# Moving weight divisions and input loads within the first expert group of a recurrence-plus-mixture kernel

## The chip, the cores and the metric

The kernel runs on one core of a Trainium2 chip. The metric is the device time of one execution in microseconds. Three runs of the kernel before took 970.49, 967.85 and 964.76 us, a median of 967.85 us.

The core's engines have their own instruction queues, which run in order: PE (TensorE, the matrix engine), DVE (VectorE), ACT (ScalarE), POOL (GpSimd) and SP (SyncE, which here only issues DMAs). They wait for each other through semaphores. DMAs are issued by SP (queue q1 in the profile) and by POOL (queue q0).

## The reference

Two blocks follow each other. The first is a gated linear recurrence over 768 steps for 4 batches and 8 heads of size 48; its output, put into rows of 384, goes to a mixture of four experts with plain weights.

```python
for t in range(S):
    state = alpha[:, :, t, :, None] * state + np.einsum('bhd,bhe->bhde', k[:, :, t], v[:, :, t])
    y[:, :, t] = np.einsum('bhd,bhde->bhe', q[:, :, t], state)
x = y.transpose(0, 2, 1, 3).reshape(B * S, H * D)          # 3072 x 384
p = domain_probs / (domain_probs.sum(-1, keepdims=True) + 1e-09)
for e in range(E):                                          # 4 experts
    h = np.maximum(x @ w1[e], 0.0)                          # 384 -> 1024
    out += p[:, e:e + 1] * (h @ w2[e])                      # 1024 -> 384
```

## The kernel before

**Units and groups.** The 3072 rows are 24 units of 128 tokens (4 batches times 6 blocks of the sequence). A unit's recurrence is done as attention over pairs of tokens, in seven levels (`attention`, L531 on): transposes of alpha, k and q on PE (`turned`, L336), copies of them on ACT (L548, L556), products of the levels on PE (L622, L698, L703), with ACT (L585, L594, L614) and DVE (L601, L603, L615) preparing each level from the one before, then the result (`yps`, L743) and the new state (`sps`, L776), for which the keys are turned back (transpose L336, copy `AT<-tp` L760). The first unit has its own function, `first_unit`, which keeps its seven stages of queries and keys in tiles that later hold weights: `places` cuts the four `w1` and four `w1s` tiles into 16 of them.

Units are put in groups: the first has 2, then come five of 4 and a last one of 2. For each group and each expert, `up` makes the hidden rows with w1 (L864 or L870) in eight steps `fc`, and `down` makes the output rows with w2 (L956). The attention of the next group runs between these matmuls. In the first group the experts go round by one (`real`): expert 1, 2, 3, then 0.

**Weights in two parts.** From the third expert of the first group on, matmuls use a rounded type, and every weight and activation is the sum of a top and a rest: three matmuls instead of one. A weight's *division* (`split_piece`) takes a raw piece of 384 KB: ACT makes the top (L294, 128x768), DVE subtracts it to give the rest (L296, 128x768), then POOL stores the two to DRAM (`kept`, L302, 768 KB for w1), from where later groups load them. The third part is a short copy that POOL loads straight from the weights, converting on the way (`load_short`, L234: `w1s` for w1, `w` for w2). The store is left out for the pieces of w2 that are divided in the first group. There are four pieces (`NQ`) to each weight of each expert.

**What sets the order.** The program is written out by hand (`manual_schedule`): the order in which the functions run is the order on every queue. Three helpers thread work into it:

- `making` is a queue of divisions. Each call of `background()`, one after each step of `up` and every few matmuls of `down`, moves every running division on by one `yield` and starts one more (at most four run).
- `BEATS`, `deal` and `advance` say at which share of a unit's time slot each of its 18 steps is issued; for the second group the last five beats have values of their own. The third of these is the beat of turning the keys back.
- `load` and `load_piece` issue the inputs of a unit and the raw weights on SP at the places where they are called.

**The parts that the change touches, as they stand before.** In `first_unit`, the third unit's alpha is loaded after the first unit's keys are copied, then piece 0 of the first w1, k, piece 1, q, pieces 2 and 3. At the first step of `up` for the first expert, SP issues four pieces of w2 and then `p_all`, the probabilities. The last expert's w1 is divided in the second layer of the third expert (`down(0, 2)`, two pieces for each of two units), followed there by pieces 0 and 1 of its w2; pieces 2 and 3 of that w2 are divided at steps 0 and 2 of its own first layer (`up(0, 3)`). The raw w2 for it (tile `raw`) is loaded at the end of `up(0, 2)`. In time, `up(0, 2)` runs from about 78 to 91 us, `down(0, 2)` to 106, `up(0, 3)` to 120 and `down(0, 3)` to 134.

Of the kernel before, what the change touches and what calls it, by code (L numbers as in the profile page):

```python
# [10 lines left out]
F32 = mybir.dt.float32  # L11
# [9 lines left out]
def kernel(  # L21
# [40 lines left out]
    E, DM, F = moe_w1.shape  # L62
    P = 128
    NCB = S // P
    NP = H // 2
# [6 lines left out]
    NQ = 4  # L72
# [11 lines left out]
    n = np.arange(QUAD)[None, :]  # L84
# [67 lines left out]
    making = deque()  # L152
# [5 lines left out]
    shared = {}  # L158
# [56 lines left out]
    def second(rest):  # L215
        return wts.tile([P, 1 if rest else 2, KC * QF], F32R, name="w2r" if rest else "w2", bufs=NQ)
# [6 lines left out]
    def first_short():  # L223
        return wts.tile([P, KC * QF], F32R, name="w1s", bufs=AHEAD)

    def whole_piece(l, i):
        e, c = divmod(i % (E * NQ), NQ)
        e = real(i // (E * NQ), e)
        if l == 0:
            return moe_w1[e].rearrange("(c p) f -> p c f", p=P)[:, :, c * QF:(c + 1) * QF]  # L230
        return moe_w2[e].rearrange("(c p) d -> p c d", p=P)[:, c * FPQ:(c + 1) * FPQ]
# [4 lines left out]
    def load_piece(l, i, beside=False, rest=False):  # L236
        if i >= E * NQ * LAST:
            return
        gi, k = divmod(i, E * NQ)
        e, c = divmod(k, NQ)  # L240
        if gi > l and not (l == 1 and fresh(gi, e)):
            if l == 0:
                w, short = wt[l][i] = first_parts(), first_short()
                nc.sync.dma_start(out=w.bitcast(F32), in_=kept[l][k])
                casts.append((beat[0], lambda: load_short(l, i, short)))
                return
            w = second(rest)
            nc.sync.dma_start(out=w[:, :1].bitcast(F32), in_=kept[l][k][:, 1:] if rest else kept[l][k][:, :1])
            if not rest:
                casts.append((beat[0], lambda: load_short(l, i, w[:, 1])))  # L250
            wt[l].setdefault(i, []).append(w)
            return
        if l == 1 and gi == 0 and not beside:
            return
        if l == 0:

            if e == 0:
                shared[c] = second(True)[:, 0], second(False)[:, 1]
            w = shared[c][e % 2].bitcast(F32)
        elif gi > 0 or e == 1:  # L260
            if c == 0:
                shared["w2"] = hid.tile([P, NQ, KC * QF], F32, name="raw2", bufs=1)
            w = shared["w2"][:, c]
        else:
            w = hidden[c][:, 0].rearrange("p f n -> p (f n)")[:, :KC * QF].bitcast(F32)
        wt[l][i] = w
        nc.sync.dma_start(out=w.rearrange("p (c n) -> p c n", c=(KC, FPQ)[l]), in_=whole_piece(l, i))
# [5 lines left out]
    def split_piece(l, i):  # L273
        gi, k = divmod(i, E * NQ)
        whole = wt[l][i]
        if i >= E * NQ:
            ws = wt[l][i] = [second(False), second(True)]
            top, rest = (w[:, 0] for w in ws)
            if k < NQ:
                load_short(1, i, ws[0][:, 1])  # L280
            else:
                nc.gpsimd.tensor_copy(out=ws[0][:, 1], in_=whole)
        else:
            ws = [first_parts()]
            top, rest = (ws[0][:, part] for part in range(2))
            if k >= PLAIN * NQ:
                if not shorts:
                    ask_short(i)
                short = shorts.popleft()
                for at in [i, i + NQ] if k // NQ == E - 1 else [i]:  # L290
                    wt[0][at] = ws[0], short
                    ready.add(at)

        nc.scalar.activation(out=top, in_=whole, func=ACT.Copy, scale=LIFT)  # L294
        yield
        nc.vector.tensor_sub(rest, whole, top.bitcast(F32))  # L296
        if (gi, k // NQ) != (1, 0):
            yield
            to = kept[l][real(gi, k // NQ) * NQ + k % NQ]
            for part, w in enumerate(ws):  # L300
                n = 2 - l
                nc.gpsimd.dma_start(out=to[:, part:part + n], in_=w[:, :n].bitcast(F32))  # L302
# [36 lines left out]
    def first_unit(fill, other):  # L339
# [3 lines left out]
        places = []  # L343
        for t in [first_parts().rearrange("p t x -> p (t x)") for _ in range(AHEAD)] + [first_short() for _ in range(AHEAD)]:
            places += [t[:, i * NP * P:(i + 1) * NP * P].bitcast(F32).rearrange("p (a n) -> p a n", n=P)
                       for i in range(t.shape[1] // (NP * P))]
        place_of = iter(places)
        AT = work.tile([P, NP, P], F32, name="AT")
        QTs = [work.tile([P, NP, P], F32, name="QT")] + [next(place_of) for _ in range(6)]
# [47 lines left out]
        def products(li, outs):  # L397
            each = QUAD // LEVELS[li]
            qv = halves(QTs[li], LEVELS[li])
            scored(outs, KTs[li], lambda p, i, s: qv[rows[i], p, each * s:each * (s + 1), 1, :])  # L400
# [24 lines left out]
        next_q(0)  # L425
        tk = turned(pair(rk))
        nc.scalar.copy(out=KTs[0], in_=tk)
        load(2, "a")
        load_piece(0, 0)
        load(2, "k")  # L430
        load_piece(0, 1)
        same_q(1)
        same_k(0)
        dec(1)
# [19 lines left out]
        second = two("near2", P, tag="g", bufs=4)  # L454
# [4 lines left out]
        same_q(4)  # L459
        next_k(3)  # L460
        same_k(3)
        load(2, "q")
        for i in range(NQ // 2, NQ):
            load_piece(0, i)
        products(3, part(second, QUAD))
        take(0, part(first, 0))
        same_q(5)
        next_q(5)
# [6 lines left out]
        fill(1, DM)  # L475
        third = two("sc", HALF, tag="sc")
        products(4, part(third, 0))
        far = ps.tile([P, NP, HALF], F32, name="far0", tag="g", bufs=4)
        for p in range(NP):
            for i in range(2):  # L480
# [338 lines left out]
    def up(gi, e, fc, slots=None):  # L819
        n = len(groups[gi]) * P  # L820
# [7 lines left out]
        if gi == fc == 0 and begins and e not in (1, E - 1):  # L828
            for k in range(NQ):
                load_piece(1, e * NQ + k, beside=True)  # L830
            if e == 0:
                nc.sync.dma_start(out=p_all, in_=moe_domain_probs.rearrange("(n p) e -> p n e", p=P))
        beside = BESIDE[(gi, e) == (1, 0)]
        if fresh(gi, e) and fc in beside and begins:
            making.append(split_piece(1, first_piece(gi, e) + beside[fc]))
# [3 lines left out]
            split_x(0, fc - (FCH - 4), slice(0, len(groups[0])))  # L839
        if gi == 0 and 0 < e < PLAIN and fc in SPLIT_AT:  # L840
            making.append(split_piece(0, e * NQ + SPLIT_AT[fc]))
        if gi == 0 and e == E - 1 and fc in (0, 2):
            making.append(split_piece(1, E * NQ + 2 + fc // 2))
        if gi == 0 and e + 1 < E and fc == FCH // 2 and begins:
            for k in range(NQ if e + 1 < E - 1 else 0):
                load_piece(0, (e + 1) * NQ + k)
# [34 lines left out]
        background()  # L881
        if f == FPQ - 1 and ends:
            if gi == 0:
                for k in range(NQ if e == E - 2 and c == NQ - 1 else 0):
                    load_piece(1, E * NQ + k)
            elif gi != LAST - 1:
                del wt[0][i]
                load_piece(0, i + AHEAD)
            while late:
                load_piece(1, late.popleft(), rest=True)  # L890
            while stores:
                stores.popleft()()
# [9 lines left out]
    def down(gi, e, slots, between):  # L902
# [3 lines left out]
        tiles = range(FCH)  # L906
        if gi == e == 0 and slots[0] == 1:
            making.extend(split_piece(0, first + NQ + k) for k in range(2))
        if gi == 0 and 0 < e < E - 1:
            making.extend(split_piece(0, first + NQ + 2 * slots[0] + k) for k in range(2))  # L910
        if gi == 0 and e == E - 2 and slots[0] == 1:
            making.extend(split_piece(1, E * NQ + k) for k in range(NQ // 2))
        if gi == 0 and e == 1 and slots[0] == 0:
            for k in range(NQ):
                load_piece(0, (E - 1) * NQ + k)
# [84 lines left out]
    def deal():  # L1000
# [16 lines left out]
        for gis in [*([gi] for gi in range(1, LAST - 1)), [LAST - 1, LAST]]:  # L1017
# [9 lines left out]
            for k in range(n):  # L1027
                u = sum(map(len, groups[:gi])) + k
                end = due - (n - 1 - k) * space
                begin = max(end - 2 * space, ends[-2])  # L1030
                ends.append(end)
                run = runs[u] if u < len(runs) else attention(u)
                beats = BEATS if gi > 1 else BEATS[:13] + ([0.66, 0.68, 0.72, 0.78, 0.79] if k < n - 1 else [0.66, 0.69, 0.8, 0.86, 0.87])
                times.append([begin + (end - begin) * beat for beat in beats])

                for j in range(1, len(BEATS)):
                    ahead = {4: 12, 7: 14, 13: 16}.get(j)
                    free_at = times[-2][ahead] + 0.5 if ahead and times[:-1] else 0.0
                    if j == 8 and times[:-1]:
                        before, at = times[-2], times[-1][j]  # L1040
                        if abs(at - before[16]) < 2.5:
                            before[16] = min(before[16], max(before[15] + 2.0, at - 5.0))
                            free_at = before[16] + 5.0
                    times[-1][j] = max(times[-1][j], times[-1][j - 1] + 0.2, free_at)
                runs_at.append((u, run))
# [100 lines left out]
```

## Time and profile before

| | |
|---|---|
| runs | 964.76, 967.85, 970.49 us, median 967.85 |
| the profiled execution | 965.28 us, its span 963.5 us |
| mean granted clock of PE | 0.998 |
| PE busy | 951.5 us, 99% of the span |
| DVE, ACT, POOL busy | 532.7, 420.5, 249.4 us |
| DMA | 251.20 MB, 261 GB/s over the span |

The profile's times are in microseconds from the first instruction. The chain of work that ended last runs over PE for 95% of the span and over DMA for 2%. Its part of the first 140 us is 21.6% L956, 15.7% L864, 8.2% the DMA of `w` and 6.8% L870. In an answer on waits, a line has the engine and the line that waited, what it waited for, and then the total, the number of times and the longest. In an answer by stage, each engine has its busy time and, in brackets, its instructions. Lines of DMA issues end with the median time from issue to landing; the lines of q0 and q1 have packets, MB and the share of 16 engines' time. In a list in order of time, a line starts with the start and the duration.

### The profile page before, as it was taken

The page shows a single profiled execution, that of the slowest core. Times are in us where ns is not written, and L with a number is a line of the kernel's source. Part 1 is how long each engine was busy: PE and PEld are TensorE (multiplying, and loading weights), DVE is VectorE, ACT ScalarE, POOL GpSimd, SP SyncE. Part 2 cuts the span into 40 slices and gives each one's busy share as a digit, 9 for nine tenths or more (in the row PEclk, how much of TensorE's full clock was granted, in tenths as well). Part 3 has the DMA queues.
Part 4 walks back from the last instruction along what each step waited for, and adds up shares of the span by engine and source line. Part 5 has one row for each costly group of instructions (what it writes and reads, how often), then busy time and mean ns, then how long its engine had stood idle before and what let it go on. Part 6 is the DMA issues. An engine that isn't in the chain of part 4 may idle for free.

```text
span 963.5 us, 24984 instructions
## 1 busy us (share of the span) xinstructions
PE 951.5 (99%) x10316; PEld 853.9 (89%) x10316; DVE 532.7 (55%) x1138; ACT 420.5 (44%) x978; POOL 249.4 (26%) x407
## 2 busy tenths in 40 slices
PE   8999999999999999999999999999999999999998
PEld 7777789898998988989989889899898899999998
DVE  6776877778587555655646456646764312221312
ACT  5787756536445444344344343555435222021111
POOL 3212413344244412313312222223221202020200
PEclk9999999999999999999999999999999999999999
DMA  9999967999899999999999899999997609192921
GB/s 229 268 338 320 326 149 207 283 319 302 210 358 332 331 321 314 293 307 291 296 300 267 264 305 301 343 253 290 305 283 263 230 2 348 45 322 71 301 92 50
DMA packets 217728, 251.20 MB, mean 261 GB/s; under 512 B 95344, under 2 KB 187376, under 8 KB 217616
## 3 DMA queue, kind: packets, MB, share of 16 engines
q1 hardware_dynamic: 158800, 160.02, 56.8%
q0 software_dynamic: 58368, 89.27, 32.7%
q8 instruction: 81, 1.33, 0.6%
q10 hardware_dynamic: 448, 0.32, 0.1%
q14 instruction: 31, 0.25, 0.1%
HBM read 219.69 MB, written 29.88 MB: 259 GB/s over the span
## 4 chain that ended last, share of the span: by engine, by line
PE 95%; DMA 2%; ACT 1%; issue 1%; POOL 0%; DVE 0%; SPq 0%; ACTq 0%; POOLq 0%
PE ops L956 42%; PE one L870 39%; PE yps L743 4%; PE sc L622 3%; PE one L864 2%; PE tp L336 2%; PE sc L698 1%; DMA w<-in_moe_w_dram 1%; PE sps L776 1%; DMA sk<-in_k_dram 1%; PE sc L703 1%; DMA sa<-in_alpha_dram 0%; PE sc L395 0%; ACT odd L585 0%; ACT w L294 0%
## 5 line engine op out<-in xcount | busy, mean ns | idle before, releaser
L956 PE MATMUL ops<-w,hT 128*128 128x384 f32 x1440 | 261.6, 339 | 2.2 <-DMA w<-in_moe_w_dram 2.1
L870 PE MATMUL one<-xT,w 128*128 128x512 f32 (+1 forms) x1104 | 262.0, 373 | 1.1 <-DVE hT L896 1.1
L956 PEld LDWEIGHTS ops<-w,hT 128*128 128x128 f32 x1440 | 249.0, 188 | 5.8 <-DMA w<-in_moe_w_dram 2.7
L875 ACT ACTIVATE hT<-one 128x512 fp32r<-128x512 f32 (+1 forms) x208 | 112.0, 541 | 283.2 <-PE one L870 282.1
L870 PEld LDWEIGHTS one<-xT,w 128*128 128x128 f32 x1104 | 196.5, 188 | 39.0 <-DVE hT L896 1.3
L896 DVE SCALAR_TENSOR_TENSOR hT<-one,hT 128x512 fp32r<-128x512 f32 (+1 forms) x208 | 128.3, 620 | 174.3 <-ACT hT L875 173.9
L870 PE MATMUL one<-xT,w1s 128*128 128x512 f32 (+1 forms) x552 | 149.7, 379 | 0.0
L234 POOL DMA_DIRECT2D w1s<-in_moe_w_dram x84 | 65.9, 784 | 259.8 <-PE one L870 254.1
L956 PE MATMUL ops<-w2r,hT 128*128 128x384 f32 x720 | 131.9, 338 | 0.0
L956 PEld LDWEIGHTS ops<-w2r,hT 128*128 128x128 f32 x720 | 125.6, 189 | 0.4 <-issue 0.2
L870 PEld LDWEIGHTS one<-xT,w1s 128*128 128x128 f32 x552 | 96.5, 188 | 16.0 <-DVE hT L896 0.4
L594 ACT COPY qb<-QT 64x256 f32<-64x256 f32 x230 | 92.5, 402 | 32.8 <-DVE QT L601 31.0
L601 DVE TENSOR_TENSOR QT<-QT,AT 128x256 f32<-128x256 f32 x158 | 70.6, 447 | 36.8 <-ACT qb L594 27.9
L978 DVE SCALAR_TENSOR_TENSOR acc<-ops,p_all,acc 128x384 f32<-128x384 f32 x66 | 39.8, 613 | 85.8 <-PE ops L956 85.1
L632 DVE COPY_PREDICATED near<-masks,sc 128x128 f32<-128x128 uint8 x115 | 40.9, 356 | 63.7 <-PE sc L622 61.8
L234 POOL DMA_DIRECT2D w<-in_moe_w_dram x68 | 49.1, 724 | 96.9 <-PE ops L956 81.0
L615 DVE TENSOR_TENSOR KT<-KT,AT 128x256 f32<-128x256 f32 x161 | 71.8, 446 | 0.0
L721 POOL COPY lat<-near 32x256 f32<-32x256 f32 x92 | 45.6, 496 | 98.5 <-DVE near L632 93.1
L614 ACT COPY KT<-KT 128x256 f32<-128x256 f32 x115 | 47.2, 411 | 5.3 <-PE sc L622 2.6
L585 ACT ACTIVATE odd<-QT,ident 64x256 f32<-64x256 f32 x36 | 18.9, 524 | 68.6 <-DVE QT L543 68.3
L603 DVE TENSOR_TENSOR AT<-AT 128x256 f32<-128x256 f32 (+1 forms) x138 | 43.0, 312 | 4.7
L786 POOL TENSOR_TENSOR st<-st,dec 64x192 f32<-64x192 f32 x32 | 17.3, 540 | 104.6 <-PE yps L743 103.3
(144 smaller groups left out, 932.0 us busy)
## 6 DMA issues: line engine op xcount, KB each, us to landing
w<-kept SPq DMA_DIRECT2D x76, 768.0 KB, 7.7
w1s<-in_moe_w_dram POOLq DMA_DIRECT2D x84, 384.0 KB, 8.7
w<-in_moe_w_dram POOLq DMA_DIRECT2D x68, 384.0 KB, 9.1
w<-kept SPq DMA_DIRECT2D x60, 384.0 KB, 7.1
w2r<-kept SPq DMA_DIRECT2D x60, 384.0 KB, 8.1
kept<-w POOLq DMA_DIRECT2D x16, 768.0 KB, 7.9
raw<-in_moe_w_dram SPq DMA_DIRECT2D x24, 384.0 KB, 8.5
kept<-w POOLq DMA_DIRECT2D x16, 384.0 KB, 7.7
```

The lines of the kernel that those rows point to most:

```text
L234: nc.gpsimd.dma_start(out=out.rearrange("p (c n) -> p c n", c=(KC, FPQ)[l]), in_=whole_piece(l, i))
L594: nc.scalar.copy(out=qb[rows, :, i, :].rearrange("p a (b r) -> p a b r", r=m), in_=qv[rows])
L601: nc.vector.tensor_mul(qv, qv, spread(dv[:, :, :, 0], m))
L603: nc.vector.tensor_mul(dec, dv[:, :, :, 0], dv[:, :, :, 1])
L614: nc.scalar.copy(out=new[:, :, :, 1, :], in_=old[:, :, :, 1, :])
L615: nc.vector.tensor_mul(new[:, :, :, 0, :], old[:, :, :, 0, :], spread(halved(decs[li])[:, :, :, 1], m))
L632: nc.vector.copy_predicated(near.rearrange("p a (b two r) -> p a b two r", two=2, r=m)[:, :, :, 1, :], mk.unsqueeze(1).broadcast_to([P, H, ...
L721: nc.gpsimd.tensor_copy(out=lat[rows, :, rows], in_=near[rows])
L870: nc.tensor.matmul(one, lhsT=short[:, kc] if part == 1 else w[:, part // 2, kc], rhs=x_part(gi, part % 2, kc)[:, lo:hi], start=(part == pa ...
L875: nc.scalar.activation(out=parts[0], in_=one, func=ACT.Relu)
L896: nc.vector.scalar_tensor_tensor(out=low, in0=x, scalar=0.0, in1=top.bitcast(F32), op0=ALU.max, op1=ALU.subtract)
L956: nc.tensor.matmul(sums[slot], lhsT=h, rhs=w, start=(n == begins[slot]), stop=(n == ends[slot]))
```

## The change

- `raw_homes` sets apart the eight tiles in which the raw w1 of the first two experts lie, before the first unit begins; places 1 to 3 of the first unit (its queries after the second, third and fourth stage) now lie in three of them instead of the `w1` tiles. Pieces 1, 2 and 3 of the first w1 are loaded when the products that read these places have been issued.
- Alpha, k and q of the third unit are loaded at the first step of `up(0, 0)`, behind `p_all`.
- In `up(0, 2)`, steps 3, 5 and 7 each put a division of the last expert's w1 (pieces 0, 1 and 2) into `making`. `down(0, 2)` then has piece 3 and the w2 pieces 0, 1 and 2; `up(0, 3)` has w2 piece 3.
- The four raw pieces of that w2 are loaded after the second step of `up(0, 2)` instead of the eighth. On SP they thereby come before k, q and v of a unit that they followed.
- The stores of the last expert's w1 are issued one `background()` later.
- The beat of turning the keys back is 0.684 instead of 0.72 for all but the last unit of the second group.

```diff
+    def raw_homes():
+        for c in range(NQ):
+            shared[c] = second(True)[:, 0], second(False)[:, 1]
...
         if l == 0:
-            if e == 0:
-                shared[c] = second(True)[:, 0], second(False)[:, 1]
             w = shared[c][e % 2].bitcast(F32)
...
         if (gi, k // NQ) != (1, 0):
-            yield
+            for _ in range(1 + (l == 0 and k // NQ == E - 1)):
+                yield
...
+        raw_homes()
+        for c in range(1, NQ):
+            places[c] = shared[c][0][:, :NP * P].bitcast(F32).rearrange("p (a n) -> p a n", n=P)
         place_of = iter(places)
...
         nc.scalar.copy(out=KTs[0], in_=tk)
-        load(2, "a")
         load_piece(0, 0)
-        load(2, "k")
-        load_piece(0, 1)
         same_q(1)
...
-        load(2, "q")
-        for i in range(NQ // 2, NQ):
-            load_piece(0, i)
+        load_piece(0, 1)
         products(3, part(second, QUAD))
+        load_piece(0, 2)
         take(0, part(first, 0))
...
         products(4, part(third, 0))
+        load_piece(0, 3)
...
                 nc.sync.dma_start(out=p_all, in_=moe_domain_probs.rearrange("(n p) e -> p n e", p=P))
+                load(2, "akq")
...
-        if gi == 0 and e == E - 1 and fc in (0, 2):
-            making.append(split_piece(1, E * NQ + 2 + fc // 2))
+        if gi == 0 and e == E - 2 and fc in (3, 5, 7):
+            making.append(split_piece(0, (E - 1) * NQ + fc // 2 - 1))
+        if gi == 0 and e == E - 1 and fc == 0:
+            making.append(split_piece(1, E * NQ + NQ - 1))
...
             if gi == 0:
-                for k in range(NQ if e == E - 2 and c == NQ - 1 else 0):
+                for k in range(NQ if e == E - 2 and c == 0 else 0):
                     load_piece(1, E * NQ + k)
...
-        if gi == 0 and 0 < e < E - 1:
+        if gi == 0 and e == 1:
             making.extend(split_piece(0, first + NQ + 2 * slots[0] + k) for k in range(2))
+        if gi == 0 and e == E - 2 and slots[0] == 0:
+            making.extend((split_piece(0, E * NQ - 1), split_piece(1, E * NQ)))
         if gi == 0 and e == E - 2 and slots[0] == 1:
-            making.extend(split_piece(1, E * NQ + k) for k in range(NQ // 2))
+            making.extend(split_piece(1, E * NQ + k) for k in (1, 2))
...
-                beats = BEATS if gi > 1 else BEATS[:13] + ([0.66, 0.68, 0.72, 0.78, 0.79] if k < n - 1 else [0.66, 0.69, 0.8, 0.86, 0.87])
+                beats = BEATS if gi > 1 else BEATS[:13] + ([0.66, 0.68, 0.684, 0.78, 0.79] if k < n - 1 else [0.66, 0.69, 0.8, 0.86, 0.87])
```

## The prediction

> **What bounds the kernel now.** I read the page first: TensorE (PE) is busy for all but 12 of 963.5 us, so the change can win back idle time and clock, not work.
>
> ```profile
> span 963.5 us, 24984 instructions
> PE 951.5 (99%) x10316; PEld 853.9 (89%) x10316; DVE 532.7 (55%) x1138; ACT 420.5 (44%) x978; POOL 249.4 (26%) x407
> ```
>
> Then the waits of PE alone, for the whole span. The three that lie where the diff works are these: the second layer of the first group's last expert waits for the short copies of w2, the first layer before it waits for a hidden tile, and one state product waits for the turned keys.
>
> ```profile
> PE ops L956 <- DMA w<-in_moe_w_dram: 2.1, 2, 1.5
> ...
> PE one L870 <- DVE hT L896: 1.1, 1, 1.1
> ...
> PE sps L776 <- ACT AT L760: 0.4, 1, 0.4
> ```
>
> Then busy time by stage. The columns after the stretch are its length, PE, PEld, DVE, ACT and POOL busy, then granted clock, DMA share and GB/s. PE is idle for 3.2 us in the first stretch, and the clock is halved for the 3.4 us after it.
>
> ```profile
> 113.00:124.30 11.30, 8.12 (x143) 7.10 (x142) 11.03 (x30) 8.92 (x22) 1.90 (x3) 1.00 1.12 330
> 124.30:127.70 3.40, 3.26 (x10) 2.39 (x8) 3.37 (x6) 0.01 (x1) 0.00 (x0) 0.50 0.43 98
> ```
>
> Last, the queue of loads on SP between 78 and 98 us, because the diff moves four loads inside it. I read the issue of 6.69 us as one that stood waiting for room in the queue.
>
> ```profile
> 78.59 1.23 SPq L201 DMA_DIRECT2D sa<-in_alpha_dram  x1
> 81.04 6.69 SPq L201 DMA_DIRECT2D sk<-in_k_dram  x1
> 88.23 3.67 SPq L201 DMA_DIRECT2D sq<-in_q_dram  x1
> 92.01 2.98 SPq L201 DMA_DIRECT2D rv<-in_v_dram  x1
> 95.05 2.23 SPq L267 DMA_DIRECT2D raw<-in_moe_w_dram  x4
> ```
>
> The DMA view of 85 to 91 us says why: the POOL queue (q0, stores and short copies) fills the engines, and SP's queue (q1) gets at most a packet for each of theirs, and its packets are small. This sk took 14.8 us to land.
>
> ```profile
> q0 software_dynamic: 861, 2.07, 97.0%
> q1 hardware_dynamic: 745, 0.21, 16.1%
> ...
> sk<-in_k_dram SPq DMA_DIRECT2D x1, 192.0 KB, 14.8
> ```
>
> The lines of the transposes (L336) say when PE wants that load: from 98.9 us. The sk that was issued at 81.04 landed at 81.04 + 14.8 = 95.8, so it has 3.0 us to spare.
>
> ```profile
> L336 PE MATMUL tp<-ident,sk x4: 272/272/273, 98.9 to 99.2; 128*128 128x128 f32 x4
> ```
>
> **The change part by part.** The numbers are differences to the profiled execution, which took 965.28 us (span 963.5 and 1.8 around it). It lies 2.57 us under the median of the runs, 967.85.
>
> *Start (0 to 60 us): 0.* The third unit's alpha, k and q leave the places between the pieces of w1 and go behind p_all. p_all is issued at 19.49 and lands 6.2 us later, at 25.7; three loads of this kind in a row landed about 1 us apart at the start (8.5, 9.1, 10.5). So the third unit's inputs land near 29; its first transpose on PE stands at 34.42. If that cover of 5.4 us were gone, its cost would be the overshoot alone. The pieces of w1 now wait for the products that read the places in them. The four issues stood at 9.06, 10.96, 13.35 and 15.03, and the products they wait for run from 10.13 to about 14.6, so none gets later, and their first use is at 19.5. On SP the second expert's four pieces, its raw w2 and the v behind them are passed by three loads: 3 us later than 32.3, 36.5 and 37.5, with uses at 49.6, 64 and 66.
>
> *Turned keys and divisions in the first layer of the third expert (78 to 92): +0.45.* The shifted beat moves the transpose of the keys nine L870 matmuls (1.1 us) ahead and its copy L760 (0.58) ahead of one L873 (0.39). But a division (L294, 0.84 us) now stands in ScalarE's queue before it. ScalarE ran without a gap from 83.51 to the copy at 87.89, so the copy comes 0.84 - 0.39 = 0.45 later, and so does the state product L776, which already waited for it. The 0.4 us wait therefore grows instead of going. Two more L294 and three subtractions L296 on VectorE (0.95 each) follow in the same unit's chain. Queued by hand with the rows of before, the third set of pairs for L622 (qb) is ready near 93.0 and PE comes to it near 93.2: no second wait, by a small margin. Bounds: 0 if ScalarE catches up, 5.4 (three of each in series) if nothing overlaps. I take 0.45, near the lower one, since VectorE is idle for 3.34 us before 87.6 in that stretch.
>
> *Raw w2 of the rotated first expert (384 KB x4) issued ahead of sk, sq and v: +5.7.* Before, those four went at 95.05, behind sk. Now they stand behind sa, so sk stands behind 1.57 MB. They find the POOL queue busier too: the divisions now made early send two stores (768 KB), two w1s and one w2 short copy between 88.6 and 94.6, 2.75 MB in a stretch where the POOL queue had run dry by 95. From 91.0, when the last of the pieces ahead of sa landed, 0.30 + 2.75 MB of POOL's and 1.57 MB of raw stand before sk. At 364 GB/s (the mean of 114 to 121, when both queues were full) these 4.62 MB take 12.7 us: 103.7, and the rest of sa and sk itself as small packets 1.3 us: 105.0. PE is there at 98.88 + 0.45 = 99.3, so it waits 5.7 us. Lower bound: q1 is not held up by the stores at all, sa lands at 95.1 as before, raw passes at the 349 GB/s of 97.5 to 101.5 in 4.5 us, sk 0.7 later, 100.3: a wait of 1.0. Upper bound: the 303 GB/s of 80 to 100, 15.2 us, and 1.7: 107.9, a wait of 8.6. I take 105, since in every stretch where both queues were full the q1 load landed only when POOL's had run out: the v issued at 110.38 landed at 125.5, the last w2 copy at 125.1.
>
> *Clock after that wait: +1.7.* In the one place where PE stood idle, for 1.45 and 0.60 us with 0.6 us of work between, the clock was then at 0.50 for 3.4 us, which costs half of it. I take the same here. The Trainium skill (TensorE: Matmul & The Clock Gate, section on why this matters for your kernels) says that gaps under about 3 us keep the clock; this trace disagrees, 2.05 us of idle in 2.7 us were enough. By the rule a wait at the lower bound would cost no clock, by the row it may; at 5.7 us both give the drop.
>
> *Behind sk on POOL.* POOL's memset of sk waits for it and for the dot product that also reads sq, so the third and fourth store and three w2 copies are issued from about 108.5 to 115 instead of 102 to 114. They are 2.75 MB now instead of 5.5, and land near 121 to 122. PE then begins the second layer at 119.5 + 0.45 + 5.7 + 1.7 - 1.1 = 126.2. So they are hidden by some 4 us; without that cover the old 2.1 us wait and its clock come back.
>
> *Gone in the last expert (113 to 128): -4.9.* The w2 wait 2.1, its half clock 1.7, and the hidden tile's 1.1: of the divisions that filled ScalarE and VectorE between 103 and 119, three L294 fewer are left. Next late there is nothing that I see: the attention chain that feeds L622 at 116.1 has fewer of them in its way.
>
> Sum: 0 + 0.45 + 5.7 + 1.7 - 4.9 = +3.0 us: 968.2 in a profiled execution, 970.9 as a median, 0.3% above the one shown. I call no difference what is within 0.5% (4.8 us), about the spread of the three runs.
>
> **The rivals.** (a) *sk comes in time.* q1 gets more of the engines than in 85 to 91, raw passes before the stores, sk lands by 100.3 or earlier. For it: raw went at 349 GB/s when alone. Against: the POOL queue is not empty there now. The sum is then -4.9 + 0.45 + 0 to 1.0 = -4.45 to -3.4: 963.4 to 964.4. Chance 0.17.
>
> (b) *Slower: the w2 copies are late again.* One mechanism: POOL stands at the memset of sk, and the copies behind it miss the second layer. It decides once the last of them, issued near 115, needs over 11 us; before, these needed 10.1 to 12.1. Against it: half the bytes stand ahead of them. The price is 2.1 + 1.7 on top of the sum: +6.8, 974.7; with the wait for sk at its upper bound +9.7, 977.6. Chance 0.18.
>
> (c) *The divisions in the first layer bind PE.* The chain ScalarE to VectorE to ScalarE of that unit takes up to all of 5.4 us; L622 at 92 waits. As PE then comes to sk later, only the longer of the two waits counts: with sk in time 965.28 - 4.9 + 5.4 + 2.57 = 968.4, otherwise about the forecast. Chance 0.10.
>
> **How the numbers follow.** The forecast, a wait for sk of 3 to 8.6 us and no wait at w2, has 0.55; its own range is +0.3 to +5.9, 968.2 to 973.8. With (a) at the lower end and (b) above, 963 to 976.5 leaves out the far part of (b) and some of the scatter of medians. Slower by over 0.5% (972.7) holds most of (b) and the part of the forecast with a wait over 7.5, together 0.32. Faster by over 0.5% (under 963.0) needs (a) and a little scatter: 0.10. The rest, 0.58, is within.
>
> **What would show it.** Right: a PE wait at tp L336 for DMA sk (or sa) of 4 to 8 us near 99, a half clock of 3.4 us right behind it, sk's landing over 20 us after its issue, and no wait of L956 for DMA w. The 0.4 us of L776 should be near 0.9. Wrong: tp L336 without that wait (then a), a w2 wait that is still there (b), waits of L622 for qb near 92 (c), or a wait before 60 us, which would say that the start is not free.

## The result and the profile after

The changed kernel takes 970.51 us (median of 22 runs, 968.31 to 973.89) against 967.65 us of the kernel before (22 runs, 964.76 to 970.49). The ratio is 1.0034, with a 95% interval from 1.0023 to 1.0044: by it the change costs 3.3 us (2.2 to 4.3; the medians lie 2.9 apart), inside the 0.5% that the prediction calls no difference. The forecast was 970.9 us, and +3.0 us. The profiled execution took 968.31 us (span 966.5), which is 3.03 us above the one of before.

The first lines of the page of the changed kernel: PE is busy for 950.9 us, 0.6 less than before, in a span that is 3.0 longer.

```profile
span 966.5 us, 24991 instructions
PE 950.9 (98%) x10316; PEld 854.2 (88%) x10316; DVE 533.3 (55%) x1138; ACT 420.6 (44%) x978; POOL 249.5 (26%) x407
```

The waits of PE over the whole span of the changed kernel, with total, number and longest. The code has moved down by three to eight lines: the transposes L336 are L339 now, the second layer L956 is L964, the state product L776 is L779, and the first layer L870 is L876.

```profile
PE tp L339 <- DMA sk<-in_k_dram: 7.7, 2, 7.5
...
PE sps L779 <- ACT AT L763: 0.8, 1, 0.8
```

The waits of the second layer for `w` (2.1 us) and of the first layer for a hidden tile (1.1) are gone. In their place stands one wait of 7.5 us for sk. The total in this view, 7.7 us, holds one more wait of 0.2 us, near 7 us, for the inputs of the first unit: all units share the line of the transposes, so such a total has to be taken apart by time. The wait for the turned keys has grown from 0.4 to 0.8.

Busy time by stage in the changed kernel; after the stretch come its length, PE, PEld, DVE, ACT and POOL, then the granted clock, the DMA share and GB/s.

```profile
100.00:106.00 6.00, 0.00 (x0) 0.00 (x0) 0.71 (x1) 0.00 (x0) 0.00 (x0) 0.68 0.99 241
106.00:113.00 7.00, 6.92 (x83) 4.67 (x84) 3.16 (x6) 2.88 (x6) 2.28 (x5) 0.79 0.88 242
113.00:124.30 11.30, 11.28 (x203) 10.21 (x205) 10.48 (x23) 9.58 (x25) 6.03 (x10) 1.00 1.00 255
124.30:140.00 15.70, 15.70 (x226) 15.37 (x214) 14.72 (x35) 9.86 (x27) 2.77 (x5) 1.00 0.37 83
```

For 6 us no matmul runs, and the other engines hardly work either: ACT waits for the transposes of PE, DVE for sq, and POOL for DVE. The clock is below 1.00 in the stall and in the 7 us behind it: a half clock for 2 x 0.32 x 6 = 3.8 us and for 2 x 0.21 x 7 = 2.9 us. From 113 us on PE is busy without a gap and at full clock, where before it stood for 3.2 us and then ran 3.4 us at 0.50.

SP's queue of loads in the changed kernel (start, duration):

```profile
77.70 0.53 SPq L201 DMA_DIRECT2D sa<-in_alpha_dram  x1
78.68 11.16 SPq L269 DMA_DIRECT2D raw<-in_moe_w_dram  x4
89.95 2.72 SPq L201 DMA_DIRECT2D sk<-in_k_dram  x1
```

The order is the one that the change wrote. The four raw loads keep the queue for 11.16 us, and sk is issued at 89.95 instead of 81.04. The DMA view of 88 to 106 us, in the changed kernel: the queue of POOL (q0) with packets, MB and its share of the engines' time, then issues, their size and the median time to landing. POOL's queue moves 3.80 MB here.

```profile
q0 software_dynamic: 2217, 3.80, 64.1%
...
w<-in_moe_w_dram POOLq DMA_DIRECT2D x1, 384.0 KB, 12.0
sk<-in_k_dram SPq DMA_DIRECT2D x1, 192.0 KB, 16.1
```

sk lands at 89.95 + 16.1 = 106.0. The last of the early copies on POOL is `w`, issued at 93.44, and it lands at 105.4. In order of time, PE of the changed kernel (start, busy time, and in brackets the idle time before it):

```profile
106.08 1.12 PE L339 MATMUL tp<-ident,sk 128*128 128x128 f32 x4 [7.47 <-DMA sk<-in_k_dram]
```

PE was ready for sk at 106.08 - 7.47 = 98.6.

### The profile page after: what moved, and what is told of

Its sections match the earlier page's. It is cut to its first block, busy times and chain, and to the rows that moved or that the text cites. A ratio compares the mean times of both kernels' runs of the same rounds, so it can differ in the third digit from the quotient of the medians.

```text
span 966.5 us, 24991 instructions
## 1 busy us (share of the span) xinstructions
PE 950.9 (98%) x10316; PEld 854.2 (88%) x10316; DVE 533.3 (55%) x1138; ACT 420.6 (44%) x978; POOL 249.5 (26%) x407
## 4 chain that ended last, share of the span: by engine, by line
PE 96%; DMA 2%; ACT 1%; DVE 1%; issue 0%; POOL 0%; DVEq 0%; POOLq 0%; ACTq 0%
PE ops L964 42%; PE one L876 40%; PE yps L746 4%; PE sc L625 3%; PE one L870 2%; PE tp L339 2%; DMA sk<-in_k_dram 2%; PE sc L701 1%; PE sps L779 1%; PE sc L706 1%; PE idle L1087 0%; PE y L515 0%; PE sc L401 0%; ACT odd L588 0%; POOL lat L724 0%
## 5 line engine op out<-in xcount | busy, mean ns | idle before, releaser
L876 PE MATMUL one<-xT,w 128*128 128x512 f32 (+1 forms) x1104 | 261.9, 373 | 0.0
L964 PE MATMUL ops<-w,hT 128*128 128x384 f32 x1440 | 260.0, 338 | 0.0
L964 PEld LDWEIGHTS ops<-w,hT 128*128 128x128 f32 x1440 | 248.8, 188 | 2.5 <-issue 0.2
L876 PEld LDWEIGHTS one<-xT,w 128*128 128x128 f32 x1104 | 196.5, 188 | 37.8 <-DVE hT L902 0.2
L876 PE MATMUL one<-xT,w1s 128*128 128x512 f32 (+1 forms) x552 | 149.7, 379 | 0.0
L964 PE MATMUL ops<-w2r,hT 128*128 128x384 f32 x720 | 131.2, 337 | 0.0
L964 PEld LDWEIGHTS ops<-w2r,hT 128*128 128x128 f32 x720 | 124.9, 188 | 0.4 <-issue 0.2
L876 PEld LDWEIGHTS one<-xT,w1s 128*128 128x128 f32 x552 | 96.5, 188 | 16.0 <-DVE hT L902 0.4
L238 POOL DMA_DIRECT2D w<-in_moe_w_dram x68 | 49.0, 723 | 96.4 <-PE ops L964 83.5
L789 POOL TENSOR_TENSOR st<-st,dec 64x192 f32<-64x192 f32 x32 | 17.6, 549 | 106.5 <-PE yps L746 105.3
```

The costliest lines, as they stand in the source:

```text
L238: nc.gpsimd.dma_start(out=out.rearrange("p (c n) -> p c n", c=(KC, FPQ)[l]), in_=whole_piece(l, i))
L876: nc.tensor.matmul(one, lhsT=short[:, kc] if part == 1 else w[:, part // 2, kc], rhs=x_part(gi, part % 2, kc)[:, lo:hi], start=(part == pa ...
L964: nc.tensor.matmul(sums[slot], lhsT=h, rhs=w, start=(n == begins[slot]), stop=(n == ends[slot]))
```

## The experiments

The wait for sk can come from two things that the change does at once. Theory A: the divisions made early put traffic on POOL's queue, 768 KB stores above all, and SP's small packets of sk get through only when that has run out. Theory B: the raw w2, 1.57 MB, stands ahead of sk on SP's own queue. One run puts the raw w2 back, one the stores, one both; others make one part alone in the kernel before. Each ratio below is to the kernel before, in runs on the same chip; the kernel before had medians of 965.41 us (31 runs) in the first series and 965.72 us (13 runs) in the second. All these kernels compute everything; one has extra stores that nobody reads.

### The raw w2 behind sk and sq

```diff
-                for k in range(NQ if e == E - 2 and c == 0 else 0):
+                for k in range(NQ if e == E - 2 and c == 2 else 0):
                     load_piece(1, E * NQ + k)
```

> The changed kernel with one number put otherwise: the four raw w2 pieces are issued after the sixth step of the third expert's first layer, so behind sk and sq on SP's queue. Two theories for the 7.5 us that PE waits for sk. Order: sk is late because 1.57 MB of raw stand ahead of it on its own queue; then the wait falls to 0.5 us or less, the half clock costs nothing, and the kernel takes about 965.3 + 3.0 - 7.5 - 1.5 = 959 us (ratio to the kernel before near 0.993). Traffic: sk is late because the early divisions fill POOL's queue until 104, and 1024 small packets pass at only about 100 per us while it is full; then sk lands near 100.5 to 104, the wait stays at 2.5 to 6 us and the kernel takes 962 to 968 us. I lean to a share of both: a wait of 2 to 4 us.

Measured: 964.76 us, ratio 0.9995 (0.998 to 1.0011). So against the changed kernel's +3.3 us, 3.8 are won; from the two intervals this difference is known to about 1.8 us. The waits of PE in its profiled execution, which took 967.79 us, the highest of its ten runs:

```profile
PE tp L339 <- DMA sk<-in_k_dram: 3.9, 2, 3.3
PE tp L339 <- DMA sq<-in_q_dram: 3.1, 2, 2.8
```

Only 3.3 of these 7.0 us are the wait in question. In order of time, PE of this execution:

```profile
61.15 0.63 PE L339 MATMUL tp<-ident,sq 128*128 128x128 f32 x4 [2.79 <-DMA sq<-in_q_dram]
...
104.53 1.11 PE L339 MATMUL tp<-ident,sk 128*128 128x128 f32 x4 [3.34 <-DMA sk<-in_k_dram]
```

The 2.8 us for sq stand at 61 us, for the inputs of another unit, and the rest near 6 us, for the first unit. sk is issued at 82.75, nearly as early as before (81.04), and still lands at 104.5. The order on SP is therefore not needed for the wait, and a wait of 3.3 us is within the 2.5 to 6 us that the theory of traffic expected.

### The raw w2 ahead of sk in the kernel before

```diff
-                for k in range(NQ if e == E - 2 and c == NQ - 1 else 0):
+                for k in range(NQ if e == E - 2 and c == 0 else 0):
                     load_piece(1, E * NQ + k)
```

> The kernel before with the raw w2 pieces issued after the second step of the third expert's first layer, so ahead of sk, and nothing else: POOL's queue sends nothing more than it did. Order: sk lands later by the time of raw, 1.57 MB at 349 GB/s = 4.5 us, at 100.3, and PE waits 1.0 to 1.5 us near 99; 966 to 968.5 us, the upper end if the clock falls too. Traffic: no wait for sk over 0.5 us, the same time as before within 0.1%.

Measured: 967.58 us, ratio 1.0017 (0.9997 to 1.0038): by itself the order costs 1.6 us, and the interval takes in zero. The waits of PE:

```profile
PE ops L956 <- DMA w<-in_moe_w_dram: 2.3, 3, 1.3
...
PE tp L336 <- DMA sk<-in_k_dram: 0.9, 1, 0.9
```

The wait for sk is 0.9 us when POOL's queue is empty by then, near the 1.0 to 1.5 of the theory of order. It is also near the lower bound of the prediction (1.0), which had assumed that the stores do not hold up SP's queue.

### The four stores held back

The stores of the last expert's w1 are put aside and issued at the odd steps of that expert's own first layer; the divisions stay where the change puts them.

```diff
+    held = deque()
...
-            for part, w in enumerate(ws):
-                n = 2 - l
-                nc.gpsimd.dma_start(out=to[:, part:part + n], in_=w[:, :n].bitcast(F32))
+            def store():
+                for part, w in enumerate(ws):
+                    n = 2 - l
+                    nc.gpsimd.dma_start(out=to[:, part:part + n], in_=w[:, :n].bitcast(F32))
+            if (l, gi, k // NQ) == (0, 0, E - 1):
+                held.append(store)
+            else:
+                store()
...
+        if gi == 0 and e == E - 1 and fc % 2 == 1 and held:
+            held.popleft()()
```

> The changed kernel with the four stores of the last expert's w1 (768 KB each) issued one by one at the odd steps of that expert's own first layer, instead of between 88 and 116; raw still stands ahead of sk. Order: the wait for sk falls little, to 5 us or more. Traffic: it falls to 1.5 us or less. By bytes, 1.57 MB of stores fewer before sk are 4.3 us: a wait of 3 us. A cost may come later: the stores then stand among the short copies of w2, and PE may wait 0 to 3 us for those in the last expert's second layer. 962 to 968 us.

Measured: 965.59 us, ratio 0.9996 (0.998 to 1.0012): 3.7 us are won against the changed kernel, again known to about 1.8. The waits of PE:

```profile
PE tp L347 <- DMA sk<-in_k_dram: 4.1, 2, 3.6
...
PE tp L347 <- DMA sq<-in_q_dram: 0.3, 1, 0.3
```

The wait for sk at the transposes in question is the longest of the first line, 3.6 us; the other 0.5 and the 0.3 for sq stand near 6 and 7 us, at the first unit. That is near the 3 us by bytes and between the two theories, which had 5 us or more and 1.5 or less. There is no wait for `w` although the stores now come in the last expert's first layer.

### The start alone, in the kernel before

Only `raw_homes`, the places, and the moved loads of the first unit and of the third unit's inputs are put into the kernel before:

```diff
-        load(2, "a")
         load_piece(0, 0)
-        load(2, "k")
-        load_piece(0, 1)
...
+                load(2, "akq")
...
```

> The kernel before with only the start of the changed one: the tiles set apart, places 1 to 3 in them, the pieces of w1 behind the products, the third unit's inputs behind the probabilities. If the 0.84 us that PE stood at L512 near 18 us in the kernel before, and did not in the changed one, belongs to this part, it is gone here and the kernel takes 964.4 us (ratio 0.999). If it was an accident of one execution, it is there here or it is not, and the time is the same within 0.1%.

Measured: 965.5 us, ratio 0.9997 (0.9981 to 1.0013). The waits of PE:

```profile
PE ops L959 <- DMA w<-in_moe_w_dram: 1.9, 2, 1.2
...
PE y L514 <- issue: 0.6, 1, 0.6
```

The start is worth nothing, as forecast. It also settles a gap near the start: the profile before shows 0.8 us of PE before line `y` with no releaser, and the first profile after shows none. With the new start it is there again at 0.6, and in a second execution of the changed kernel at 0.3, so it is no result of the change. But something does change with the new start. The sq of a unit of the second group, which PE wants near 59 us, took 12.6 us to land in each of the four profiled executions with the old start (12.56 to 12.65). In the nine with the new start it took from 12.6 to 18.7 us, and in two of these PE waited for it, 0.4 and 2.8 us. The median shows no cost, but single executions do; why the landing varies is open.

### Both put back

The two edits above together: stores held, raw w2 behind sk and sq (`c == 2`).

> The changed kernel with both parts put back: raw behind sk and sq, and the four stores held until the last expert's own first layer. So far raw alone ahead gave a wait of 0.9 us for sk, the traffic of POOL's queue alone 3.3 us for sk and 2.8 for sq, both together 7.5. If these two causes are all, the waits for sk and sq together fall below 1.5 us here; what is left comes from the two w1s and the one w2 short copy that are still early (1.18 MB, 3.2 us at 364 GB/s, against 3.0 us that sk had to spare). 961 to 963 us, ratio 0.994 to 0.998. If something else made sk late, the waits stay over 3 us.

Measured: 960.89 us, ratio 0.9957 (0.9941 to 0.9973), 4.2 us faster than the kernel before. The waits of PE:

```profile
PE one L886 <- DVE hT L912: 1.0, 1, 1.0
PE sps L787 <- ACT AT L771: 0.8, 1, 0.8
```

Busy time by stage of this kernel (columns as above):

```profile
98.00:112.00 14.00, 14.00 (x216) 11.22 (x215) 12.62 (x25) 11.07 (x26) 7.79 (x14) 1.00 1.16 246
112.00:124.30 12.30, 11.30 (x222) 10.63 (x222) 11.04 (x31) 7.46 (x20) 1.72 (x3) 1.00 0.92 323
124.30:140.00 15.70, 15.70 (x192) 15.49 (x191) 13.07 (x32) 10.69 (x28) 3.96 (x7) 1.00 0.69 176
```

Nothing is waited for at the transposes near 99 us, as expected if the two causes are all. Without the wait for sk only the gain is left: no wait for `w`, no half clock. The hidden tile's 1.1 us is there again (1.0 at L886), and the 0.8 of the turned keys stays. From the prediction's terms, with the hidden tile's wait kept, -2.1 - 1.7 + 0.45 = -3.35 us follows; the interval of the measured -4.2 (-5.7 to -2.6) holds it.

### Only the divisions of w1 early

As the last one, but the pieces of w2 are divided where the kernel before did it (in the second unit of `down(0, 2)`, and at steps 0 and 2 of `up(0, 3)`), and the raw w2 is loaded after step eight, as before (`c == NQ - 1`).

```diff
-        if gi == 0 and e == E - 1 and fc == 0:
-            making.append(split_piece(1, E * NQ + NQ - 1))
+        if gi == 0 and e == E - 1 and fc in (0, 2):
+            making.append(split_piece(1, E * NQ + 2 + fc // 2))
...
```

> A version meant to beat both: only the divisions of the last expert's w1 are early, their stores are held as above, the raw w2 is loaded where it was in the kernel before, and its divisions are two in the second layer and two in the first layer that follows. The w2 short copies no longer stand behind stores. Expected: waits for sk under 1 us, none of L956 for w2 short copies, so 965.4 - 3.5 to 965.4 - 5 = 960.5 to 962 us, ratio 0.995 to 0.9965. If the traffic theory is wrong and the early divisions themselves cost PE through ScalarE and VectorE, waits for qb or for hidden tiles show up and the ratio is near 1.

Measured: 961.53 us, ratio 0.9964 (0.9951 to 0.9977). The waits of PE:

```profile
PE sps L787 <- ACT AT L771: 1.3, 2, 0.8
...
PE one L886 <- DVE hT L912: 1.0, 1, 1.0
```

Neither `w` nor sk is waited for. So dividing w1 earlier and storing it later is enough for most of the gain; the kernel with the divisions of w2 moved too is 0.6 us faster by the medians, and the intervals of the two do not tell them apart.

### More stores in the kernel before

Nothing of the change is in this one. Four stores of 768 KB, to a place in DRAM that nobody reads, are issued on POOL at about 87 to 89 us.

```diff
+    idle_stores = dram.tile([P, 4, 2, KC * QF], F32, name="idle_stores")
...
+            if (gi, e, slots[0], n) == (0, E - 2, 0, FCH // 2):
+                for k in range(4):
+                    nc.gpsimd.dma_start(out=idle_stores[:, k], in_=wt[0][first_piece(gi, e) + 2 + k % 2][0].bitcast(F32))
```

> The kernel before with nothing moved, and four stores of 768 KB more on POOL's queue near 87 us, to a place in DRAM that nobody reads (they store two w1 pieces of the third expert again). Traffic: POOL's queue then runs dry at 94.9 + 3.1 MB at 364 GB/s = 103.6 instead of 94.9, and sk, with nothing new ahead of it on its own queue, lands near 100 to 103: PE waits 1.5 to 4.5 us for it (or for sa before it) near 99; 967 to 971 us. Order: sk lands as before, no wait, 965 to 966 us.

Measured: 972.07 us, ratio 1.0064 (1.0047 to 1.008), 6.2 us slower. The waits of PE:

```profile
PE tp L337 <- DMA sa<-in_alpha_dram: 3.6, 1, 3.6
PE ops L960 <- DMA w<-in_moe_w_dram: 3.2, 2, 2.6
```

Traffic of POOL alone, with every load of SP where it was, makes PE wait for the inputs: sk is issued at 81.63 and lands 22.5 us later, at 104.1. Here sa is the one that is waited for first. The time lies above the 967 to 971 us expected: the extra stores also make the wait for `w` in the last expert longer, 3.2 us instead of 2.1, so not all of the 6.2 us belongs to the inputs.

### A second execution of four kernels

By the totals of the waits, the order alone gave 0.9 us, early traffic alone 6 to 7, and both 7.7. The medians don't say that: each part put back wins 3.7 to 3.8 us, and both together 3.3 + 4.2 = 7.5. One of the two had to be off, and the profiled execution with 7.0 had been the highest of its runs. So four kernels were profiled once more. The 6.1 us and the 3.9 us that the expectations below name hold waits of other places, as does the 2.8 us for sq in the expectation of both put back; at the transposes near 100 us the first executions had waited 3.3 and 3.6 us.

> The changed kernel once more, for a second profiled execution. If the first one is typical, TensorE waits about 7.5 us for sk at the transposes and the half clock behind or in it is 3.4 or 6.8 us. A wait that differs by over 1.5 us would say that one execution is not enough to split the wait into its causes.

> The kernel with the raw w2 behind sk and sq once more. Its first profiled execution waited 6.1 us for sk and sq and took 967.79 us, 3.0 over the median of its own runs. Theory A (traffic is nearly all of it): 5 to 6 us again. Theory B (by the medians the order of raw and the early traffic are worth the same, about 3.8 us each): an execution near the median of 964.8 waits about 3 us in all.

> The kernel before with only the raw w2 ahead of sk once more. Its first profiled execution waited 0.9 us for sk, had no half clock, and was the fastest of its runs (963.73 against a median of 967.58). Theory A: 0.9 us again, and the half clock behind the wait for w2 is back. Theory B: 2 to 4 us for sk.

> The changed kernel with the four stores held once more. Its first profiled execution, at the median of its runs, waited 3.9 us for sk and sq. Both theories: 3 to 4.5 us again.

The waits of PE in the second execution of the kernel with the raw w2 behind sk and sq:

```profile
PE tp L339 <- DMA sk<-in_k_dram: 2.8, 2, 2.6
PE y L515 <- issue: 1.4, 1, 1.4
```

All executions side by side. The second column is when PE came to the transposes of sk (with more stores, of sa) and found the engine free; the waits are those at this place alone. The landings of sk are issue plus time to landing; the last POOL copy is the last one that was issued before 97 us.

```
kernel                    PE ready   PE waits   sk lands   last POOL copy   time of it
                          (us)       (us)       (us)       lands (us)       (us)
before                     98.9      none        95.8       94.9            965.28
raw ahead, in before       98.6      0.9         99.3       95.6            963.73
raw ahead, again           99.1      0.9         99.9       95.4            965.66
after                      98.6      7.5        106.0      105.4            968.31
after, again               99.4      7.1        106.5      105.7            969.05
raw behind                101.2      3.3        104.5      105.6            967.79
raw behind, again         101.4      2.6        103.9      105.5            965.85
stores held                99.2      3.6        102.7      101.9            965.58
stores held, again         99.3      3.8        103.1      102.5            967.49
both put back              98.6      none        96.1       99.8            959.98
more stores, in before     97.9      3.6        104.1      103.7            972.41
```

In both kernels with early traffic and the raw w2 ahead (after, stores held) sk lands 0.6 to 0.8 us behind POOL's last copy, in all four executions. In the two with early traffic and the raw w2 behind, it lands 1.1 and 1.6 us ahead of it. There PE came to this place some 2 to 3 us later than elsewhere, because of stalls far ahead of it (2.8 us at 61 us in the one; 1.4 us at `y` and a half clock from 20.0 to 23.4 us in the other), and POOL issued its last copy as much later (96.0 and 96.2 us instead of 93.4 and 94.3). So the landings of different executions are to be compared with PE's arrival, not with each other.

Taken so, the two executions of each kernel agree to within 0.7 us, and the waits agree with the medians within what those can tell: the raw w2 put back takes 3.8 to 4.9 us off the wait, the stores held 3.3 to 3.9, and by the medians they are worth 3.8 and 3.7. (The half clock behind each wait, which costs 1.4 to 3.0 us in these traces, is not in the waits.) Neither theory holds alone. By A the raw w2 behind should have left 5 to 6 us, by B the raw w2 ahead in the kernel before should have cost 2 to 4. The two causes add up in the landing, and PE waits only for what exceeds its cover. In the kernel before sk lands 3.0 us ahead of PE. The order alone moves it by 3.8 us against PE, the early traffic alone by 5.6 and 6.3; the sum is 9.4 to 10.1, and with both it moves by 10.1 and 10.5. By itself the order is therefore nearly hidden (0.9 us of wait), and on top of the traffic it costs all of its delay.

## Why the prediction was right

The forecast of +3.0 us came out at +3.3 (2.2 to 4.3), and its places are the ones that the profile shows: the mechanism was right. That the number came so close is in part luck, as the sum below shows. Term by term, from the profiled executions:

- **Start, 0.** Right: 0.9997 by itself. The 0.8 us gap at `y` that the first profile after lacks comes and goes. The term named the loads that are passed on SP, but not the sq of the second group that lands late in some executions; PE waited 0.4 us for it at 59 us in the second execution of the changed kernel.
- **Turned keys, +0.45.** Measured: 0.4 became 0.8 (0.9 in the second execution). Queueing ACT by hand was enough. There was no second wait at the products behind it, so rival (c), the divisions binding PE, did not happen: ACT and DVE had room.
- **Raw w2 ahead of sk, +5.7.** The mechanism was right, POOL's early traffic and the raw w2 ahead of sk, which lands when both have passed. The size was off by 1.8 us: PE waited 7.5. Of this 1.0 is the landing, 106.0 for 105.0, and 0.7 is PE, ready at 98.6 for 99.3. The landing was mis-sized by the bytes and the rate. The last raw piece landed at 105.3, 14.3 us after 91.0 and not 12.7; 4.86 MB moved in that time at 340 GB/s, where 4.62 MB at 364 GB/s (from 114 to 121 us) had been reckoned. The 0.8 us from there to sk are less than the 1.3 allowed for. The value is inside the bounds (1.0 to 8.6), nearer to the upper one. The name of the step was too narrow, though: it put under "raw w2 ahead of sk" what the stores and copies of the early divisions do as well. Its working without raw, 3.05 MB at 364 GB/s, would have put sk at 100.7 and the wait at 1.4 us; 2.6 and 3.3 were seen. The kernel with both put back lands sk at 96.1, 0.3 us from what the same working would give with 1.48 MB (91.0 + 4.1 + 1.3 = 96.4).
- **Clock, +1.7.** Measured about 1.45: the half clock lasted 6.8 us (from 102.14 to 108.97 in the trace; 3.8 + 2.9 from the stages), twice as long as assumed, but some 3.9 us of that fell into the stall, where it costs nothing, and half of the other 2.9 is lost.
- **Behind sk on POOL, hidden.** Right. The third and fourth store and the copies were issued from 108.4 to 117.3, the copies landed at 115.2, 122.1 and 124.4, and the second layer began at 127.1. The cover was 2.7 us instead of 4. Rival (b), late w2 copies, did not happen.
- **Gone in the last expert, -4.9.** Right for this kernel: the waits of 2.1 and 1.1 us and the half clock are absent. The 1.1 came out for another reason than the one given, three divisions fewer in the last expert: the kernel with both put back has the same divisions early and waits 1.0 us again, and so does the other faster kernel. The likelier reason is that in the changed kernel PE came late to that place, behind the stall; this is argued, not shown.

The sum as measured is 0 + 0.45 + 7.5 + 1.45 - 4.9 = +4.5, 1.5 above the forecast. The two spans still differ by 3.0 only, because the profiled execution of before also stood 0.8 us at `y`, and 0.95 us near 6 and 7 us for the first unit's inputs, of which 0.2 is left after. In the waits of PE in the kernel before:

```profile
PE y L512 <- issue: 0.8, 1, 0.8
PE tp L336 <- DMA sk<-in_k_dram: 0.5, 1, 0.5
PE tp L336 <- DMA sq<-in_q_dram: 0.4, 1, 0.4
```

These 1.6 us come and go between executions and are no result of the change; with them the sum is +2.9. In the profile the hit of +3.0 is thus an error of +1.5 in the terms against an accident of -1.6, and the +3.3 of the runs is the figure to hold the forecast against. Rival (a), sk in time, is what the kernel with both put back shows: -4.2, for a price worked out as -4.45 to -3.4.

What would show it wrong had been named: no wait at the transposes, a wait for `w`, for qb near 92, or one before 60 us. None of these is in the first profile; the second has the 0.4 us at 59 us. One sign was off in form: sk's landing was to come over 20 us after its issue and came 16.1 after it, since the issue itself was put off to 89.95 by the raw loads.

## What to carry to other kernels

Work that is moved earlier takes its stores along: before moving it, list what each moved step puts on every DMA queue, and look for the small load with a due time in that stretch. Here the moved work was free on its engines and its stores were not; with the first two stores held back by some 20 us and the raw load behind the small ones, 0.3% slower became 0.4% faster. When two causes are split by single profiles, set them against the medians too, and where they disagree look first at when each wait stands: a total by line adds the waits of all units, and here it took a 2.8 us wait 40 us away for a part of the effect. A load with cover hides one delay and shows the second in full, so two causes that each look small alone can cost much together.

## What the runs showed of the hardware that was not expected

**Short stalls and the clock.** The prediction took from the trace of before that 2.05 us of idle in 2.7 us halve the clock. Whether idle time does so depends on where it falls. The same stretch of the kernel before with the raw w2 ahead, in its first and then in its second profiled execution (PE in order of time):

```profile
122.32 0.62 PE L956 MATMUL ops<-w,hT 128*128 128x384 f32 x2 [1.26 <-DMA w<-in_moe_w_dram]
123.66 0.97 PE L956 MATMUL ops<-w,hT 128*128 128x384 f32 x4 [0.71 <-DMA w<-in_moe_w_dram]
```

```profile
122.86 0.62 PE L956 MATMUL ops<-w,hT 128*128 128x384 f32 x2 [1.20 <-DMA w<-in_moe_w_dram]
124.23 2.42 PE L956 MATMUL ops<-w,hT 128*128 128x384 f32 x6 [0.75 <-DMA w<-in_moe_w_dram]
```

1.26 and 0.71 us of idle (and 0.36 soon after) left the clock at 1.00, and 1.20 and 0.75 us halved it. The half clock that followed waits lasted 3.41 or 6.83 us in the profiles of this study. The Trainium skill (TensorE: Matmul & The Clock Gate, Part 1: The HAM clock gate) says that the clock is set by how busy PE was in a window of 3413 ns that runs free of the program. These rows agree with it: the durations are one and two windows.

The position of the window can be read from the traces too. In each of them the recorded clock begins a few us into the span, and every later change lies a whole number of 3.413 us behind that: in the second execution here the record begins at 5.00, and the clock falls at 124.47, 35.0 windows later. Counted on like this (the record of the first begins at 6.54), the windows around the stalls are these, again first the one and then the other; the first number after a stretch is its length, the second is PE's busy time, and the third from the end is the granted clock.

```profile
119.18:122.60 3.42, 2.16 (x13) 1.84 (x12) 3.32 (x12) 2.16 (x7) 0.00 (x0) 1.00 1.26 327
122.60:126.01 3.41, 2.33 (x12) 1.72 (x12) 3.38 (x8) 1.58 (x5) 0.00 (x0) 1.00 0.53 120
```

```profile
121.05:124.46 3.41, 1.46 (x7) 0.82 (x6) 3.31 (x13) 2.35 (x8) 0.00 (x0) 1.00 1.15 280
124.47:127.88 3.41, 3.41 (x11) 2.81 (x10) 3.38 (x6) 0.35 (x2) 0.00 (x0) 0.50 0.41 87
```

In the first execution the stalls fall into two windows with 1.26 and 1.08 us of idle, in the second into one with 1.95, and the clock is halved right behind it. Over the 13 traces of this study, all 11 windows at full clock with 1.86 us of idle or more were followed by a half clock (the end of the program aside), and none with 1.43 or less was; of the two between, one with 1.70 was and one with 1.74 was not.

**A landing set by another queue.** The same load of 192 KB took from 9.1 to 22.5 us to land, by what POOL's queue held and what stood ahead of it on its own. In seven of the eight executions of the table with early traffic or extra stores, sk landed within 1.6 us of POOL's last copy, whenever it had been issued (81.6 to 90.3 us); in the eighth, with both put back, it landed 3.7 us ahead of it.
